# Softcap attention and spectral mix on one core: the second tanh behind the first transposes' rounding, and the last output block in halves

## The chip, the cores and the metric

The kernel runs on 1 core of one Trainium2 chip. The metric is device microseconds of one execution, as the median of several runs. The engines are named as the profile names them: PE is TensorE (its weight loads are PEld), DVE is VectorE, ACT is ScalarE, POOL is GpSimd, SP is SyncE, which here issues the DMA transfers.

## The reference

Attention with a soft cap, 8 batches of 12 heads, 448 positions, 64 per head, followed by a layer that mixes positions and channels (the names with `moe_` are this layer's):

```
scores = (q @ k.T) / sqrt(64)
scores = cap * tanh(scores / cap)                  # cap = 30
attn   = exp(scores - max); attn = attn / (sum(attn) + 1e-9)
x      = attn @ v                                  # to [8, 448, 768]
theta  = x @ w_theta
zr, zi = x * cos(theta), x * sin(theta)
u      = x + w_tok_r @ zr + w_tok_i @ zi           # over positions
out    = u + max(u @ w_ch, 0)
```

All inputs and outputs are float32, up to the products with `w_theta`, the tokens' weights and `w_ch`, which the kernel makes from high and low parts.

## The kernel before, in words

Everything is kept transposed, channels on partitions and positions along the row. The heads are taken in pairs: a pair k (48 in all, 6 per batch) fills one block of 128 channels, `X[b, j]`.

The outermost loop, in `pipeline`, runs over slots s. The first 8 slots (`FIRST`) hold attention alone. After them six slots make a batch b of the second layer; `part`, 0 to 5, is the slot's place among the six. In each slot s below 48 (`live`) the kernel also does the attention of pair s, so that both kinds of work are interleaved. The program is scheduled by hand: each engine executes its instructions in the order in which the Python code emits them, and waits on semaphores where a tile isn't ready. PE, DVE, ACT and the DMA issues on SP are thus four queues, each in order. What an instruction at the head of a queue waits for delays everything behind it in that queue.

A slot goes like this:

- `qk_half(s, 0)`: the score products of the first half of the keys (PE, line 217) into the tile `s`, which has one buffer of four PSUM banks, and then their tanh (ACT, line 219) into `p`.
- `av(s - 1)`: the product with v of the pair before (line 257, into a bank of the pool `psM`), copied by ACT (line 260).
- `sums`: the row sums `r` (line 273) of the two pairs before, in a bank of `psM`; `invert` takes their reciprocal (DVE, line 296), spreads it by four DMAs (line 300), and `norm` multiplies later (line 304).
- `qk_half(s, 1)`: the second half of the scores and their tanh. The scores' buffer is the one that the first half had.
- the script of the part, a list of steps. The letters A and B are the exponentials of the two halves (line 225), a and b the additions of their parts (lines 247, 250).

The script of the third part, `part == 2`, is the one that matters here:

```
[(transp, 1), (sincos, 1), (mix, 0), (rotate, 3), (transp, 2), "A", (mix, 1), "a", (rotate, 4), (transp, 3), "B",
 (mix, 2), "b", (rotate, 5)],
```

`transp(b, j)` transposes a rotated block in seven pieces (PE, line 355) into two banks `t`; ACT copies each to `zh`, rounded (line 356), and DVE forms the remainder `zl` (line 357), which frees the bank. `mix(b, j)` accumulates 21 products of `zh` and `zl` (lines 364 to 366) in a bank `mx`, and DVE adds the result to X (line 367). `sincos` is two ACT instructions (lines 341, 342) with a load of the activation table ahead of them, and `rotate(b, j)` a multiplication on DVE (line 346). The pool `psM` has four banks for all of these.

In the third part `invert(s - 1)` is emitted after the script's first step, `transp(b, 1)`, and so is `prep(s + 1)`, which rounds the next q and k on DVE (lines 193, 194) and issues the load of those after it (line 183). In the other parts both come ahead of the script. Third parts with `live` true are the seven slots s = 10, 16, 22, 28, 34, 40 and 46; in all seven s - 1 is odd, so that `invert` has work to do.

At the end of a batch, `chan(b, m)` makes the product with `w_ch` for one output block (lines 322 to 324), and one DVE instruction takes the maximum with zero and adds (line 375); SP stores the block (line 376). The last block of the last batch is the last work of the kernel.

Of the kernel before, what the change touches and what calls it, by code (L numbers as in the profile page):

```python
# [16 lines left out]
AF = mybir.ActivationFunctionType  # L17
ALU = mybir.AluOpType

P = 128  # L20
# [12 lines left out]
WHOLE = 14  # L33
# [3 lines left out]
def softcap_attn_then_spectral_mix(ctx, tc, qk2, v, cap, w_theta, w_tok, w_ch, ident, outT):  # L37
    nc = tc.nc
    B, NP, P, _, S = qk2.shape
    D = P // 2  # L40
    CP = v.shape[2]
    NCH = S // CP
    DM = NP * P
    NJ = DM // P
    NC2 = 2 * S // P
    NS = B * NP
# [14 lines left out]
    qscale = const.tile([P, 1], F32, name="qscale")  # L61
# [20 lines left out]
    def fill(n):  # L82

        t = psM.tile([P, 512], F32, tag="m", name=f"fill{len(fills)}")
        fills.append(t)
        for _ in range(n):
            nc.tensor.matmul(t[:32, :CP], ones_sb, ones_sb[:, :1].broadcast_to([CP, CP]), start=True, stop=True)
# [77 lines left out]
    def weights(s, pos):  # L165
        for word in WEIGHTS.get((s, pos), "").split():
            step = steps[word[-3:-1], int(word[-1])]
            {">": step.load, "*": step.scale, "#": step.vscale}.get(word[0], step.split)()
# [8 lines left out]
    def load_qk(k):  # L177

        if 0 < k < WHOLE:
            raw[k] = wk.tile([P, 2, S], F32, tag=("hi", "lo")[k % 2], name=f"qk{k}", bufs=1)  # L180
        else:
            raw[k] = qk_sb
        nc.sync.dma_start(raw[k], qk2[k // NP, k % NP])

    def load_v(k):
        vt[k] = wk.tile([CP, 2, NCH, D], F32, tag="v", name=f"v{k}", bufs=2)
        nc.sync.dma_start(vt[k], v[k // NP, k % NP])
# [10 lines left out]
    def apart(k):  # L198


        return k < NP and k % 2 == 0

    def qk_half(k, half):

        sp = psS.tile([P, 2, 2, 512], F32, tag="s", name=f"s{k}_{half}")
        if apart(k):
            pp = wk.tile([CP, 2, 2, S], F32, tag="xhl", name=f"p{k}_{half}", bufs=3)
        else:
            pp = wk.tile([CP, 2, 2, S], F32, tag="p", name=f"p{k}_{half}", bufs=3)
        pt[k, half] = pp  # L210
        for i in range(2):
            ks = slice((2 * half + i) * CP, (2 * half + i + 1) * CP)
            products = ((raw, raw),) if k < WHOLE else ((hi, hi), (lo, hi), (hi, lo))
            for n, (kk, qq) in enumerate(products):
                for hh in range(2):
                    rows = slice(hh * D, (hh + 1) * D)
                    nc.tensor.matmul(sp[:CP, i, hh, :S], kk[k][rows, 1, ks], qq[k][rows, 0, :],  # L217
                                     start=n == 0, stop=n == len(products) - 1)
        nc.scalar.activation(pp, sp[:CP, :, :, :S], AF.Tanh, scale=qscale[:CP])  # L219

    def exp_half(k, half):

# [29 lines left out]
    def av(k):  # L252
        va = vt.pop(k)
        acc = psM.tile([P, 512], F32, tag="m", name=f"a{k}")
        for c in range(NCH):
            for hh in range(2):
                nc.tensor.matmul(acc[hh * D : (hh + 1) * D, :S], va[:, hh, c, :], pt[k, c // 2][:, c % 2, hh, :],  # L257
                                 start=c == 0, stop=c == NCH - 1)
        x = wk.tile([P, S], F32, tag="x", name=f"x{k}", bufs=12)
        nc.scalar.copy(x, acc[:, :S])  # L260
        X[k // NP, k % NP] = x
# [24 lines left out]
    def invert(k):  # L286

        if k % 2 == 0:
            return
        r = state.pop("r")  # L290
        ri = wk.tile([P, S], F32, tag="ri", name=f"ri{k}", bufs=1)
        if state["general"]:
            nc.vector.tensor_scalar_add(ri, r[:, :S], 1e-9)
            nc.vector.reciprocal(ri, ri)
        else:
            nc.vector.reciprocal(ri, r[:, :S])  # L296
        for n in (k - 1, k):
            bc[n] = wk.tile([P, S], F32, tag="bc", name=f"bc{n}", bufs=2)
            for i in range(2):
                nc.sync.dma_start(bc[n][i::2, :], ri[D * (n % 2) : D * (n % 2) + D, :])  # L300

    def norm(k):
        x = X[k // NP, k % NP]
        nc.vector.tensor_tensor(x, bc.pop(k), x, op=ALU.mult)
# [4 lines left out]
    def split_x(b, j, name):  # L309
        if j % 2 == 0:  # L310
            state["xhl"] = wk.tile([P, 2, 2, S], F32R, tag="xhl", name=f"{name}{b}_{j}", bufs=3)
        t = state["xhl"][:, j % 2]
        nc.scalar.copy(t[:, 0, :], X[b, j])
        nc.vector.tensor_tensor(t[:, 1, :], X[b, j], t[:, 0, :].bitcast(F32), op=ALU.subtract)
        XHL[b, j] = t

    def proj(b, wh, wl, m, name):
        acc = psM.tile([P, 512], F32, tag="m", name=f"{name}{b}_{m}")
        ms = slice(m * P, (m + 1) * P)
        for j in range(NJ):  # L320
            t = XHL[b, j]
            nc.tensor.matmul(acc[:, :S], wh[:, j, ms], t[:, 0, :], start=j == 0, stop=False)  # L322
            nc.tensor.matmul(acc[:, :S], wh[:, j, ms], t[:, 1, :], start=False, stop=False)  # L323
            nc.tensor.matmul(acc[:, :S], wl[:, j, ms], t[:, 0, :], start=False, stop=j == NJ - 1)  # L324
        return acc
# [43 lines left out]
    def chan(b, m):  # L369
        acc = proj(b, wch_h, wch_l, m, "ch")  # L370
        if m == NJ - 1 and b + 1 < B:
            for j in range(NJ):
                split_x(b + 1, j, "xs")
        x = X.pop((b, m))
        nc.vector.scalar_tensor_tensor(x, acc[:, :S], 0.0, x, op0=ALU.max, op1=ALU.add)  # L375
        nc.sync.dma_start(outT[b, m * P : (m + 1) * P, :], x)

# [13 lines left out]
    def us(b, j):  # L393
        split_x(b, j, "us")

    def pipeline(general):
        state["general"] = general
        load_v(0)
        load_qk(1)
        for step in (("tk", 0), ("tk", 1)):  # L400
            steps[step].load()

        for s in range(FIRST + 6 * B):
            k = s - 1
            b, part = divmod(s - FIRST, 6)
            live = s < NS
            start = s < FIRST
            if s == 0:
                fill(FILL["first scores"])
            if live:  # L410
                qk_half(s, 0)
            if s == 0:
                fill(FILL["half"])
            if start:
                weights(s, "a")
                exp_half(s, 0)
            if 0 <= k < NS:
                av(k)
            if not start:
                weights(s, "a")  # L420
            if not start and part == 4:
                for j in range(NJ // 2, NJ):
                    us(b, j)
            if s + 1 < NS:
                load_v(s + 1)
            if 0 <= k < NS:
                sums(k, (0,) if start else (0, 1))
                if not start and part != 2:
                    invert(k)
            if live:  # L430
                qk_half(s, 1)
            if s == 0:
                fill(FILL["slot"])
            if 0 <= k and start:
                sums(k, (1,))
            if s + 2 <= WHOLE:
                load_qk(s + 2)
            if WHOLE <= s + 1 < NS and (start or part != 2):
                prep(s + 1)
            weights(s, "b")  # L440
            if 0 <= k and start:
                invert(k)
            script = ["B", "a", "b"] if start else part_scripts(b)[part]
            for i, e in enumerate(script):
                if not start and i == len(script) - 1:
                    weights(s, "c")
                    if s % 2 == 1 and s <= NS + 1:
                        norm(s - 3)
                        norm(s - 2)
                if isinstance(e, str):  # L450
                    if live:
                        if e in "AB":
                            exp_half(s, "AB".index(e))
                        else:
                            add_half(s, "ab".index(e))
                else:
                    e[0](b, e[1])
                if part == 2 and i == 0 and not start:
                    if 0 <= k < NS:
                        invert(k)  # L460
                    if WHOLE <= s + 1 < NS:
                        prep(s + 1)
            if start:
                weights(s, "c")
                for n in {4: (0, 1), 5: (2, 3), 7: (4, 5)}.get(s, ()):
                    norm(n)
                for j in {6: range(4), 7: range(4, NJ)}.get(s, ()):
                    split_x(0, j, "xs")
# [53 lines left out]
```

## Time and profile before

| | us |
|---|---|
| median of 3 runs | 964.53 (964.43 to 966.29) |
| profiled execution, its own time | 966.27 |
| its span, first to last instruction | 964.5 |
| PE busy | 945.6 |
| DVE busy | 640.8 |
| ACT busy | 590.5 |
| mean granted PE clock | 0.997 |

A profile page gives busy time per engine, the chain of work that ended last and groups of instructions by line. In a timeline a row has the start and the duration in us, the engine, the line of the kernel, the operation, what it writes and reads, its shape, how many instructions are merged in the row, and in brackets how long the engine had been idle before it and what ended that. Matmuls are pipelined and their ends are modelled, so that neighbouring ones overlap in the records.

### The profile page before, as it was taken

To read this page: it belongs to the slowest core of one execution; us is meant where nothing else is said; L and a number is where in the kernel's file an instruction comes from. 1 tells how busy PE (TensorE), PEld (TensorE's weight loads), DVE (VectorE), ACT (ScalarE), POOL (GpSimd) and SP (SyncE) were. 2 spreads that over 40 slices of the span, in tenths; PEclk is the share of its full clock that TensorE was granted. 3 is DMA by queue.
4 is the path that set the end of the run, shared out by engine and by line. 5 is a ranking of instruction groups with operands and counts; after the bars stand their busy time and mean duration, and the time that the engine had idled before them with its cause. 6 is when DMAs were issued, how large, how long until landed. Compare 5 with 4: busy or idle time off the path is not lost.

```text
span 964.5 us, 12776 instructions
## 1 busy us (share of the span) xinstructions
PE 945.6 (98%) x5224; PEld 697.3 (72%) x5224; DVE 640.8 (66%) x877; ACT 590.5 (61%) x609; POOL 0.4 (0%) x6
## 2 busy tenths in 40 slices
PE   8999999999999999999999999999999999999997
PEld 4234766677778777777787687767777877789897
DVE  5998787885855757756766559656585576664541
ACT  6888784667654687546963578456775558722520
POOL 0000000000000000000000000000000000000000
PEclk9999999999999999999999999999999999999999
DMA  7564122330113212132122221033011321001001
GB/s 252 193 194 138 34 82 94 112 103 30 49 39 105 67 39 63 32 98 67 32 66 68 77 67 48 29 87 94 31 49 39 105 68 39 20 15 62 0 1 61
DMA packets 30739, 68.68 MB, mean 71 GB/s; under 512 B 4304, under 2 KB 16720, under 8 KB 30672
## 3 DMA queue, kind: packets, MB, share of 16 engines
q1 hardware_dynamic: 30672, 67.78, 23.0%
q8 instruction: 43, 0.70, 0.3%
q14 instruction: 24, 0.20, 0.1%
HBM read 45.74 MB, written 11.01 MB: 59 GB/s over the span
## 4 chain that ended last, share of the span: by engine, by line
PE 88%; DVE 6%; ACT 4%; issue 1%; POOL 0%; POOLq 0%
PE a L257 15%; PE s L217 14%; PE mx L364 6%; PE mx L366 6%; PE mx L365 6%; PE th L322 6%; PE ch L322 6%; PE ch L324 6%; PE th L323 6%; PE ch L323 6%; PE th L324 6%; PE t L355 3%; PE r L273 3%; ACT p L219 2%; DVE ri L296 2%
## 5 line engine op out<-in xcount | busy, mean ns | idle before, releaser
L219 ACT ACTIVATE p<-s,qscale 112x1792 f32<-112x1792 f32 x96 | 168.7, 1757 | 168.7 <-PE s L217 168.7
L225 ACT ACTIVATE p<-p,cap_sb 112x1792 f32<-112x1792 f32 x96 | 170.6, 1790 | 0.6
L257 PE MATMUL a<-p,v 112*64 112x448 f32 x768 | 154.9, 545 | 0.0
L364 PE MATMUL mx<-wtk_h,zh 128*128 128x448 f32 x336 | 126.8, 377 | 5.4 <-DVE ri L296 3.6
L366 PE MATMUL mx<-wtk_h,zl 128*128 128x448 f32 x336 | 123.6, 368 | 0.0
L365 PE MATMUL mx<-wtk_l,zh 128*128 128x448 f32 x336 | 123.5, 367 | 0.0
L257 PEld LDWEIGHTS a<-p,v 112*64 112x64 f32 x768 | 50.9, 136 | 86.9 <-issue 77.1
L322 PE MATMUL th<-xs,wth_h 128*128 128x448 f32 x288 | 106.9, 371 | 0.0
L322 PE MATMUL ch<-us,wch_h 128*128 128x448 f32 x288 | 106.8, 371 | 0.0
L324 PE MATMUL ch<-us,wch_l 128*128 128x448 f32 x288 | 105.5, 366 | 0.0
L323 PE MATMUL th<-xs,wth_h 128*128 128x448 f32 x288 | 105.4, 366 | 0.0
L323 PE MATMUL ch<-us,wch_h 128*128 128x448 f32 x288 | 105.3, 366 | 0.0
L324 PE MATMUL th<-xs,wth_l 128*128 128x448 f32 x288 | 105.3, 366 | 0.0
L250 DVE TENSOR_TENSOR ps<-ps,p 112x896 f32<-112x896 f32 x80 | 87.0, 1087 | 1.4
L296 DVE RECIPROCAL ri<-r 128x448 f32<-128x448 f32 x24 | 70.8, 2952 | 12.0 <-PE r L273 11.9
L335 DVE SCALAR_TENSOR_TENSOR g_sb<-g_sb 128x448 f32<-128x448 f32 x48 | 29.9, 624 | 65.8 <-ACT g_sb L334 65.4
L364 PEld LDWEIGHTS mx<-wtk_h,zh 128*128 128x128 f32 x336 | 63.6, 189 | 11.9 <-issue 5.0
L357 DVE TENSOR_TENSOR zl<-t,zh 128x512 fp32r<-128x512 f32 x96 | 55.2, 616 | 24.5 <-ACT zh L356 24.5
L375 DVE SCALAR_TENSOR_TENSOR x<-ch,x 128x448 f32<-128x448 f32 x48 | 29.8, 620 | 59.0 <-PE ch L324 59.0
L366 PEld LDWEIGHTS mx<-wtk_h,zl 128*128 128x128 f32 x336 | 63.5, 189 | 5.4
L365 PEld LDWEIGHTS mx<-wtk_l,zh 128*128 128x128 f32 x336 | 63.7, 190 | 4.9
L322 PEld LDWEIGHTS ch<-us,wch_h 128*128 128x128 f32 x288 | 54.1, 188 | 9.6 <-issue 4.6
(75 smaller groups left out, 1377.8 us busy)
## 6 DMA issues: line engine op xcount, KB each, us to landing
qk_sb<-in_qk SPq DMA_DIRECT2D x35, 448.0 KB, 3.4
v<-in_v SPq DMA_DIRECT2D x48, 224.0 KB, 2.5
bc<-ri SPq DMA_DIRECT2D x96, 112.0 KB, 2.3
out_dram<-x SPq DMA_DIRECT2D x48, 224.0 KB, 1.9
qk<-in_qk SPq DMA_DIRECT2D x13, 448.0 KB, 3.4
g_sb<-in_wth SPq DMA_DIRECT2D x6, 768.0 KB, 5.4
g_sb<-in_wch SPq DMA_DIRECT2D x6, 768.0 KB, 4.7
swk_raw<-in_wtok SPq DMA_DIRECT2D x7, 448.0 KB, 4.1
```

What stands on the lines that cost most here:

```text
L217: nc.tensor.matmul(sp[:CP, i, hh, :S], kk[k][rows, 1, ks], qq[k][rows, 0, :], start=n == 0, stop=n == len(products) - 1)
L219: nc.scalar.activation(pp, sp[:CP, :, :, :S], AF.Tanh, scale=qscale[:CP])
L225: nc.scalar.activation(pp, pp, AF.Exp, scale=cap_sb[:CP])
L250: nc.vector.tensor_tensor(pst[k], pst[k], pt[k, 1][:, i], op=ALU.add)
L257: nc.tensor.matmul(acc[hh * D : (hh + 1) * D, :S], va[:, hh, c, :], pt[k, c // 2][:, c % 2, hh, :], start=c == 0, stop=c == NCH - 1)
L296: nc.vector.reciprocal(ri, r[:, :S])
L322: nc.tensor.matmul(acc[:, :S], wh[:, j, ms], t[:, 0, :], start=j == 0, stop=False)
L323: nc.tensor.matmul(acc[:, :S], wh[:, j, ms], t[:, 1, :], start=False, stop=False)
L324: nc.tensor.matmul(acc[:, :S], wl[:, j, ms], t[:, 0, :], start=False, stop=j == NJ - 1)
L364: nc.tensor.matmul(acc[:, :S], zh[:, c, :], wtk_h[:, c, :], start=c == 0, stop=False)
L365: nc.tensor.matmul(acc[:, :S], zh[:, c, :], wtk_l[:, c, :], start=False, stop=False)
L366: nc.tensor.matmul(acc[:, :S], zl[:, c, :], wtk_h[:, c, :], start=False, stop=c == NC2 - 1)
```

## The change

Two edits. First, `qk_half` no longer emits the tanh: it returns a function that does. The first half calls it at once, and so does the second half in most slots. In third parts (`late`) the tanh of the second half is emitted after the script's first step, so that in ACT's queue it stands behind the two copies of `transp(b, 1)`; `invert` and `prep` stay behind it in the emitted order. Second, the very last output block (b = 7, m = 5) is finished in two halves of 224 columns: DVE's instruction becomes two, the first half is stored by SP and the second by a DMA issued from ACT.

```
     def qk_half(k, half):
...
-        nc.scalar.activation(pp, sp[:CP, :, :, :S], AF.Tanh, scale=qscale[:CP])
+        return lambda: nc.scalar.activation(pp, sp[:CP, :, :, :S], AF.Tanh, scale=qscale[:CP])
...
     def chan(b, m):
...
-        nc.vector.scalar_tensor_tensor(x, acc[:, :S], 0.0, x, op0=ALU.max, op1=ALU.add)
-        nc.sync.dma_start(outT[b, m * P : (m + 1) * P, :], x)
+
+        parts = 2 if (b, m) == (B - 1, NJ - 1) else 1
+        for i in range(parts):
+            cs = slice(i * S // parts, (i + 1) * S // parts)
+            nc.vector.scalar_tensor_tensor(x[:, cs], acc[:, cs], 0.0, x[:, cs], op0=ALU.max, op1=ALU.add)
+            (nc.scalar if i else nc.sync).dma_start(outT[b, m * P : (m + 1) * P, cs], x[:, cs])
...
             if live:
-                qk_half(s, 0)
+                qk_half(s, 0)()
...
+            late = not start and part == 2
             if live:
-                qk_half(s, 1)
+                tanh = qk_half(s, 1)
+                if not late:
+                    tanh()
...
-            if WHOLE <= s + 1 < NS and (start or part != 2):
+            if WHOLE <= s + 1 < NS and (not late):
                 prep(s + 1)
...
-                if part == 2 and i == 0 and not start:
+                if late and i == 0:
+                    if live:
+                        tanh()
                     if 0 <= k < NS:
                         invert(k)
                     if WHOLE <= s + 1 < NS:
```

## The prediction

> **What bounds the kernel now.** I read the page first, for the engine that fills the span.
>
> ```profile
> span 964.5 us, 12776 instructions
> ...
> PE 945.6 (98%) x5224; PEld 697.3 (72%) x5224; DVE 640.8 (66%) x877; ACT 590.5 (61%) x609; POOL 0.4 (0%) x6
> ```
>
> TensorE (PE) is busy nearly throughout. A new order on ScalarE (ACT) can pay only where PE stands still, so I read next the list of waits.
>
> ```profile
> PE mx L364 <- DVE ri L296: 3.6, 7, 0.5
> ```
>
> Its columns are total us, times and longest: PE waits seven times, 0.51 us each, for the reciprocal of line 296. The change touches seven slots: s = 10, 16, ..., 46, the third parts that still have scores to compute. I then read the chain of waits in the slot s = 16 (start us, us, what).
>
> ```profile
> 245.17 0.94 ACT p L219
> 246.11 0.72 issue
> 246.83 0.58 ACT zh L356
> 247.41 0.02 issue
> 247.44 1.16 DVE zl L357 x2
> 248.59 2.87 DVE ri L296
> 251.46 0.14 issue
> 251.60 0.44 PE mx L364
> ```
>
> It goes from the tanh of the second scores (line 219) to the rounding of the transposes (356), their remainder on VectorE (DVE, 357), the reciprocal, and then PE's mix 1. By the order of releases mix 1 gets the PSUM bank that held the row sums, free only after the reciprocal has read it. The tanh heads this chain and has nothing to do with it: it is there because ACT works in order. The timeline of the same slot, engine by engine (ACT, DVE, PE), gives the slack.
>
> ```profile
> 245.17 1.76 ACT L219 ACTIVATE p<-s,qscale 112x1792 f32<-112x1792 f32 x1 [1.76 <-PE s L217]
> 246.83 0.95 ACT L356 CAST zh<-t 128x512 fp32r<-128x512 f32 x2
> 247.80 1.28 ACT L341 ACT_TABLE_LOAD   x1
> 249.09 1.42 ACT L341 ACTIVATE g_sb<-g_sb,quarter 128x1344 f32<-128x1344 f32 x1
> 250.42 1.31 ACT L342 ACTIVATE g_sb<-g_sb 128x1344 f32<-128x1344 f32 x1
> ...
> 256.59 0.97 ACT L356 CAST zh<-t 128x512 fp32r<-128x512 f32 x2 [0.91 <-PE t L355]
> ```
>
> ```profile
> 245.30 1.08 DVE L346 TENSOR_TENSOR g_sb<-g_sb,x 128x896 f32<-128x896 f32 x1
> 247.44 1.16 DVE L357 TENSOR_TENSOR zl<-t,zh 128x512 fp32r<-128x512 f32 x2 [1.05 <-ACT zh L356]
> 248.51 2.95 DVE L296 RECIPROCAL ri<-r 128x448 f32<-128x448 f32 x1
> ...
> 253.51 1.08 DVE L346 TENSOR_TENSOR g_sb<-g_sb,x 128x896 f32<-128x896 f32 x1
> 254.51 1.15 DVE L357 TENSOR_TENSOR zl<-t,zh 128x512 fp32r<-128x512 f32 x2
> ```
>
> ```profile
> 245.06 0.98 PE L355 MATMUL t<-ident_sb,g_sb 128*128 128x128 f32 x7
> ...
> 250.16 0.93 PE L355 MATMUL t<-ident_sb,g_sb 128*128 128x128 f32 x7
> ...
> 255.95 0.93 PE L355 MATMUL t<-ident_sb,g_sb 128*128 128x128 f32 x7
> 256.63 0.45 PE L364 MATMUL mx<-wtk_h,zh 128*128 128x448 f32 x1
> ```
>
> **What PE loses per slot.** Transposes followed by a mix without a wait: 256.63 - 255.95 = 0.68 us from start to start. With the wait: 251.60 - 250.16 = 1.44. The loss is 0.76, more than the 0.51 of shown idle, because modelled matmul ends cover part of it.
>
> **Part 1: tanh behind the rounding.** No instruction is added: the same tanh runs once per slot, after both zh copies instead of ahead of them.
>
> How early the copies can start: an unhindered copy follows its transposes by 256.59 - 255.95 = 0.64. The first transposes start at 245.06, so the copy comes at 245.70 instead of 246.83, 1.13 earlier. Its remainder could come 1.13 earlier too, but DVE is in the rotation of line 346 until 246.38; the row says DVE idled 1.05 for the copy, so it gains 1.05. The reciprocal follows directly and now ends at 251.46 - 1.05 = 250.41; with the 0.14 of issue mix 1 may go at 250.55. Unhindered it would go at 250.16 + 0.68 = 250.84. The wait is gone with 0.29 to spare: gain 0.76.
>
> In s = 10 DVE has more to do and less to win.
>
> ```profile
> 130.82 1.16 DVE L357 TENSOR_TENSOR zl<-t,zh 128x512 fp32r<-128x512 f32 x2 [0.48 <-ACT zh L356]
> ```
>
> Only 0.48 of idle lies ahead of the remainder there, so the reciprocal and mix 1 come 0.48 earlier. I take the other six as the slot s = 16. Sum: 6 x 0.76 + 0.48 = 5.04 us.
>
> What gets late is the tanh. It starts at 245.70 + 0.97 (pitch of the two copies, 247.80 - 246.83) = 246.67 instead of 245.17. Behind it on ACT stand the table load, cosine, sine, the copies of transposes 2 and the exponentials. With the pitches of the rows, 1.66 for the tanh (246.83 - 245.17), 1.29, 1.33 and 1.31 for the last, the sine ends at 252.26 instead of 251.73, 0.53 later. Its consumer, rotation 3 on DVE at 253.51, itself moves up 1.06 to 252.45: it still finds the sine done, by 0.2. PE has more slack: rotation 3 may start as late as 255.87 (new mix 2) - 0.14 - 1.15 (remainder) - 1.00 (rotation pitch, 254.51 - 253.51) = 253.58 before mix 2 waits for its remainder. The cover is 253.58 - 252.26 = 1.32 us; beyond it PE would wait at mix 2. The tanh's own readers are later still: it now ends near 248.4, while exponential B comes behind the copies of 256.59, and the score bank's next writer is the next slot. DVE's rounding of the next q and k behind the reciprocal, SP's stores of the reciprocal and the q-k load behind them are issued earlier by up to the 1.05; nothing in SP's queue is added or passed, and POOL has no part in it. The bank order is unchanged, since the tanh takes and frees no bank of that pool.
>
> **Part 2: the last block in halves.** VectorE's one operation becomes two of 224 columns; the first half is stored by SP, the second by ACT's queue. Every issue that the page lists is SP's, so a store from ACT is bounded by SP's. The rows are the timeline's end, the last store's time from issue to landing, the group of the same kind of operation at 768 columns, the page's row of a 112 KB transfer, and the shortest, median and longest landing of the last six stores.
>
> ```profile
> 959.41 0.62 DVE L375 SCALAR_TENSOR_TENSOR x<-ch,x 128x448 f32<-128x448 f32 x1 [3.04 <-PE ch L324]
> 960.07 0.33 SPq L376 DMA_DIRECT2D out_dram<-x  x1
> ```
>
> ```profile
> DMA to landing us min/median/max: 2.6/2.6/2.6
> ```
>
> ```profile
> L121 DVE SCALAR_TENSOR_TENSOR g_sb<-g_sb 128x768 int32<-128x768 int32 x12 | 11.5, 961 | 0.4
> ```
>
> ```profile
> bc<-ri SPq DMA_DIRECT2D x96, 112.0 KB, 2.3
> ```
>
> ```profile
> DMA to landing us min/median/max: 1.9/2.2/3.7
> ```
>
> From 0.62 us at 448 columns to 0.961 at 768: 1.07 ns a column, so 0.38 for 224. Two of them end at 959.41 + 0.76 = 960.17 instead of 960.03, 0.14 later. With the same 0.04 to the issue, the second half is issued at 960.21. With the 2.3 of the 112 KB row it lands at 962.51, against 960.07 + 2.6 = 962.67 now: gain 0.16. The ends: with 1.9 it lands at 962.11 (-0.6), with 3.7 at 963.91 (+1.2). I take 2.3 because the size is the same. The first half, issued 0.24 earlier, is hidden behind the second.
>
> The Trainium skill (DMA: Bandwidth & Descriptors, Rules for kernel authors) speaks against this part: two halves of a transfer share the same 16 DMA engines, and a second issuing engine saves only issue time, so "Don't bother". Its halves are halves of the partitions; here they are columns, but the engines are shared all the same. By that rule this part gives 0 and the whole change 5.0. No run here shows yet which.
>
> **The sum.** 5.04 + 0.16 = 5.2 us. The profiled execution took 966.27 for a span of 964.5 and becomes about 961.1 for a span of 959.3. The median of the runs is 964.53, 1.7 below the profiled execution's time (one of the three runs was 966.29), so the forecast of the median is 964.53 - 5.2 = 959.3. Should the median fall on an execution of the longer kind, it is 961.1.
>
> **Rivals.**
>
> Partial gain: only the shown idle comes back, 7 x 0.51 = 3.6, because the other 0.25 per slot is PE's own restart, or because the copies come later after their transposes than 0.64. With the tail as forecast this gives 960.8, with its worst end, +1.2, it is 962.1. For it: the 0.29 to spare at mix 1 is small. Against it: transposes and mix without a wait stand 0.68 apart, all restart included.
>
> No change: mix 1 waits for something else that comes at the same time, so that only the tail moves: 964.4. For it: a wait is put down to what came last, and another could stand just behind. Against: what else mix 1 reads, the remainder of the first transposes, is done 2.87 us before (it ends where the reciprocal starts), and the sine on ACT, at 251.73, ends after mix 1 has started.
>
> Slower: the tanh between the copies and the sine brings two additional table loads per slot on ACT.
>
> ```profile
> L341 ACT ACT_TABLE_LOAD x15 | 19.2, 1283 | 0.3
> L225 ACT ACT_TABLE_LOAD x14 | 18.0, 1283 | 0.3
> ```
>
> Two loads of 1.283 put the sine's end at 252.26 + 2.57 = 254.83, the remainder of transposes 2 at 255.83 to 256.98 and mix 2 at 257.12, 0.49 after its place now; in seven slots 3.4, so 964.53 + 3.4 - 0.16 = 967.8. It decides once ACT is late by more than 254.34 - 252.26 = 2.1 us in each slot (254.34 is the start of rotation 3 that lets mix 2 go at 256.63, as now). Against it: the sines and what follows them have 15 and 14 loads in the whole kernel, so tanh, copy and exponential need none between them, and the new order has copies and tanh together ahead of the sine's load.
>
> **How the numbers follow.** Forecast 0.80 (its own range, with the tail's ends, 958.9 to 960.7), partial gain 0.11, no change 0.04, slower 0.05. A difference under 0.2% (1.9 us) can't be told from none in this kernel. Forecast and partial gain are both faster by more than that: 0.91; same 0.04; slower 0.05. The range runs from 957.8, a little more gain than the 0.76 per slot, to 961.9: it takes in a median of the longer kind and most of the partial gain.
>
> **What would show it.** Right: no wait of mix 1 (364) on the reciprocal; the copy (356) of the first transposes 0.64 after their start, the tanh behind it; the remainder right behind rotation 2, and the reciprocal behind it; transposes 2 to mix 1 at 0.68; as many table loads as before; the two last issues about 0.37 apart and the span's end 4.2 us after the last VectorE operation, now 4.5 (964.5 - 960.03). Wrong would be: PE waiting on line 357 or 346 in these slots (ACT's cover gone), a copy that comes over 0.3 later after its transposes, or a last store that takes 3.7.

## The result and the profile after

The kernel after takes 959.57 us in the median of 4 runs (959.22 to 959.83), beside 965.41 for the kernel before on the same chip (4 runs, 964.43 to 966.36): ratio 0.9936, interval 0.9922 to 0.995. The prediction was 959.3. The profiled span went from 964.5 to 958.1 us, 6.4 us, where the sum had 5.2; the difference is a second matter, told below.

The list of waits of the kernel after has one row left for mix products on PE; the seven waits on the reciprocal (296) are gone.

```profile
PE mx L364 <- DVE zl L357: 1.8, 1, 1.8
```

The timeline of the slot s = 16, as ACT, DVE and PE lines, shows the new order.

```profile
245.56 0.97 ACT L356 CAST zh<-t 128x512 fp32r<-128x512 f32 x2 [2.35 <-PE t L355]
246.41 1.77 ACT L219 ACTIVATE p<-s,qscale 112x1792 f32<-112x1792 f32 x1
248.20 1.28 ACT L341 ACT_TABLE_LOAD   x1
249.49 1.42 ACT L341 ACTIVATE g_sb<-g_sb,quarter 128x1344 f32<-128x1344 f32 x1
250.82 1.31 ACT L342 ACTIVATE g_sb<-g_sb 128x1344 f32<-128x1344 f32 x1
```

```profile
245.10 1.08 DVE L346 TENSOR_TENSOR g_sb<-g_sb,x 128x896 f32<-128x896 f32 x1
246.18 1.16 DVE L357 TENSOR_TENSOR zl<-t,zh 128x512 fp32r<-128x512 f32 x2
...
247.25 2.95 DVE L296 RECIPROCAL ri<-r 128x448 f32<-128x448 f32 x1
...
252.26 1.08 DVE L346 TENSOR_TENSOR g_sb<-g_sb,x 128x896 f32<-128x896 f32 x1
```

```profile
244.87 0.98 PE L355 MATMUL t<-ident_sb,g_sb 128*128 128x128 f32 x7
...
249.96 0.93 PE L355 MATMUL t<-ident_sb,g_sb 128*128 128x128 f32 x7
250.65 0.45 PE L364 MATMUL mx<-wtk_h,zh 128*128 128x448 f32 x1
...
255.01 0.93 PE L355 MATMUL t<-ident_sb,g_sb 128*128 128x128 f32 x7
255.69 0.45 PE L364 MATMUL mx<-wtk_h,zh 128*128 128x448 f32 x1
```

The copies start 0.69 us after their transposes (245.56 - 244.87) and the tanh follows. The remainder (357) no longer has an idle time in brackets: it comes right behind rotation 2. The reciprocal ends at 250.20, and mix 1 follows transposes 2 by 0.69 (250.65 - 249.96) where it was 1.44: the gain is 0.75 in this slot. In s = 10 it is less:

```profile
133.94 0.93 PE L355 MATMUL t<-ident_sb,g_sb 128*128 128x128 f32 x7
134.82 0.45 PE L364 MATMUL mx<-wtk_h,zh 128*128 128x448 f32 x1
```

0.88 from start to start there, 0.57 less than the 1.45 before (133.54 to 134.99). The end of the kernel, as the timeline and the last stores' time to landing show it:

```profile
953.09 0.69 DVE L379 SCALAR_TENSOR_TENSOR x<-ch,x 128x224 f32<-128x224 f32 x2 [3.04 <-PE ch L324]
953.51 0.33 SPq L380 DMA_DIRECT2D out_dram<-x  x1
953.81 0.38 ACTq L380 DMA_DIRECT2D out_dram<-x  x1
```

```profile
DMA to landing us min/median/max: 2.7/2.7/2.7
```

From VectorE's last start to the span's end it takes 958.1 - 953.09 = 5.0 us, and took 964.5 - 959.41 = 5.1.

**Where 6.4 us went.** PE's place in the two traces, at points that can be compared (transposes of s = 10 in; third transposes of s = 46; third transposes of s = 52, in the last batch), before in the first fence and after in the second:

```profile
128.44 0.98 PE L355 MATMUL t<-ident_sb,g_sb 128*128 128x128 f32 x7
...
829.45 0.92 PE L355 MATMUL t<-ident_sb,g_sb 128*128 128x128 f32 x7
...
912.75 0.93 PE L355 MATMUL t<-ident_sb,g_sb 128*128 128x128 f32 x7
```

```profile
128.84 0.98 PE L355 MATMUL t<-ident_sb,g_sb 128*128 128x128 f32 x7
...
824.68 0.93 PE L355 MATMUL t<-ident_sb,g_sb 128*128 128x128 f32 x7
...
906.42 0.93 PE L355 MATMUL t<-ident_sb,g_sb 128*128 128x128 f32 x7
```

The kernel after comes into the first of the seven slots 0.40 late; its trace first records the full clock at 10.69 us, the one before at 9.87, and 0.82 us more at half clock would cost 0.41 (an estimate). At the end of the last slot it is 4.77 early: the slots gave 5.17 (predicted 5.04). Between the last two points it gains another 1.56, in a stretch that the change does not touch. The tail gives 0.1. The 1.56 is a stretch of half clock in the trace before. In the table of windows of the kernel before (us, then busy time of PE, PEld, DVE, ACT and POOL with their instructions, granted clock, DMA):

```profile
904.16:907.58 3.42, 1.59 (x12) 1.30 (x11) 2.82 (x6) 3.42 (x7) 0.00 (x0) 1.00 0.00 0
907.58:910.99 3.41, 3.41 (x11) 3.02 (x10) 1.72 (x3) 1.33 (x2) 0.00 (x0) 0.50 0.00 0
910.99:914.40 3.41, 3.41 (x22) 3.17 (x21) 1.45 (x2) 0.97 (x2) 0.00 (x0) 1.00 0.00 0
```

PE stands idle for 1.83 us in the first window, ahead of mix 0 of s = 52 (the row of the first fence, in both kernels). In the second the granted clock is 0.50, and half as many matmuls run (11 instead of 22). In the profile of the kernel after the same idle runs from 900.21 to 902.04, and the clock stays at 1.00:

```profile
898.15:901.56 3.41, 2.06 (x17) 1.74 (x15) 2.42 (x5) 2.81 (x7) 0.00 (x0) 1.00 0.00 0
901.56:904.97 3.41, 2.93 (x14) 2.72 (x15) 2.96 (x5) 2.57 (x3) 0.00 (x0) 1.00 0.00 0
```

The changes of clock in a trace lie on a grid of 3.41 us. In the kernel before the idle lay whole within one interval of it; here a boundary at 901.56 cuts it. So 1.56 of the 6.4 us are the luck of these two executions and not of the change. The two times of the kernel before, which the prediction had noticed (964.5 and 966.3) without a cause, lie about as far apart.

### The profile page after: what moved, and what is told of

Same layout as the page of the kernel before. It is cut to its first block, busy times and chain, and to the rows that moved or that the text cites. A ratio compares the mean times of both kernels' runs of the same rounds, so it can differ in the third digit from the quotient of the medians.

```text
span 958.1 us, 12772 instructions
## 1 busy us (share of the span) xinstructions
PE 942.8 (98%) x5224; PEld 696.7 (73%) x5224; DVE 641.7 (67%) x878; ACT 589.8 (62%) x609; POOL 0.4 (0%) x6
## 4 chain that ended last, share of the span: by engine, by line
PE 93%; ACT 3%; DVE 3%; issue 1%; POOL 0%; POOLq 0%
PE a L257 15%; PE s L217 14%; PE mx L364 7%; PE mx L366 7%; PE mx L365 7%; PE th L322 6%; PE ch L322 6%; PE ch L324 6%; PE th L324 6%; PE th L323 6%; PE ch L323 6%; PE t L355 4%; PE r L273 3%; ACT p L219 2%; PE fill L87 1%
## 5 line engine op out<-in xcount | busy, mean ns | idle before, releaser
L379 DVE SCALAR_TENSOR_TENSOR x<-ch,x 128x448 f32<-128x448 f32 (+1 forms) x49 | 29.8, 611 | 59.1 <-PE ch L324 59.1
L356 ACT CAST zh<-t 128x512 fp32r<-128x512 f32 x96 | 45.8, 532 | 31.1 <-PE t L355 31.1
```

## The experiments

**The tanh alone.** The kernel after with the last block stored whole:

```
-        parts = 2 if (b, m) == (B - 1, NJ - 1) else 1
+        parts = 1
```

> Only the tanh is moved; the last block is stored whole. My theory (the wait of mix 1 on the reciprocal cost 0.76 us in six slots and about 0.5 in one, and the halves are worth 0.1): 4.9 to 5.1 us under the kernel before where both run at full granted clock, so 959.4 to 959.7, no wait of line 364 on line 296, and the span's end 5.08 us after VectorE's last operation starts, as before. Rival, the halves bring the 1.2 us by which the profiled spans differ beyond my sum: 960.5 or more.

Measured 960.59 (5 runs, 959.33 to 961.27), ratio to the kernel before 0.9947 (0.9933 to 0.9961). Three runs with a mean granted clock of 0.997 took 960.59 to 961.27, and the profiled one of these has a half clock window in its trace. One, at 0.999, took 959.81, a tenth above the forecast; one, at 0.998, took 959.33 and can't be placed without its trace. So the median alone (960.59, just where the rival begins) decides little, and the trace decides: transposes of s = 10 start at 127.86 and the third ones of s = 46 at 823.76, 0.58 and 5.69 ahead of the kernel before. The seven slots gave 5.11 without the halves, and 5.17 with them. There is no wait of 364 on 296. The span ends 5.2 us after VectorE's last start (953.76, span 959.0).

**The halves alone.** The kernel before, with the changed end of `chan`.

> Only the last block is cut in halves; the tanh stays ahead of the copies. My theory: within 0.2 us of the kernel before (964.4 or so at full clock), VectorE's last start to the span's end 5.0 us instead of 5.08. Rival, the halves bring 1.2 us: 963.3.

Measured 966.16 (11 runs, 964.39 to 966.64), ratio 1.0006 (0.9997 to 1.0016), against a kernel before at 966.0 (23 runs, 962.95 to 966.65). The rival's 1.2 us is excluded; a gain of 0.16 is neither shown nor excluded, since the interval reaches from 0.3 us less to 1.5 us more, and ten of the eleven runs have the lower clock (0.997) beside thirteen of the 23. The span ends 5.2 us after VectorE's last start (957.50, span 962.7). In all ten profiles of this document that time is 5.08 to 5.20 with the store whole (three kernels, median 5.10) and 4.73 to 5.22 with it in halves (seven kernels, median 4.96): if the halves gain a tenth, it is smaller than the scatter.

**The tanh twice.** The kernel after, with the late tanh executed twice:

```
                     if live:
                         tanh()
+                        tanh()
```

> The kernel after, with the late tanh executed twice in the seven slots (the second writes the same values). ACT is 1.66 us later in each. My cover arithmetic on the trace after: rotation 3 may start up to 253.40 in the slot s = 16, the sine ends at 252.13, so the cover is 1.27; 1.66 exceeds it by 0.4, PE waits 0.4 us at mix 2 in six slots and 0.2 in s = 10: 2.6 us over the kernel after, about 962.1, with waits of line 364 on line 357. Rival, ACT has slack to spare in these slots (61% busy): no change, 959.5. Other rival, everything of ACT is on the path: 7 x 1.66 = 11.6, 971.

Measured 962.65 (7 runs, 962.31 to 963.51). That is 3.1 us over the kernel after's 959.57, where 2.6 was expected. The profiled execution took 962.31 with a span of 960.5, only 2.4 us over the kernel after's 958.1, both without a half clock window; but it comes into the slot s = 10 0.74 ahead of the kernel after (128.10 and 128.84) and leaves the third transposes of s = 46 2.15 behind it (826.83 and 824.68), so that the seven slots lost 2.9 us up to there, and with the last slot's wait at mix 2, which stands behind that point, 3.3. In the slot s = 16:

```profile
253.54 1.09 DVE L346 TENSOR_TENSOR g_sb<-g_sb,x 128x896 f32<-128x896 f32 x1 [1.61 <-ACT g_sb L342]
254.55 1.15 DVE L357 TENSOR_TENSOR zl<-t,zh 128x512 fp32r<-128x512 f32 x2
254.68 0.42 PEld L355 LDWEIGHTS t<-ident_sb,g_sb 128*128 128x128 f32 x4 [0.30 <-DVE g_sb L346]
254.69 1.15 PE L355 MATMUL t<-ident_sb,g_sb 128*128 128x128 f32 x7
...
255.75 0.19 PEld L364 LDWEIGHTS mx<-wtk_h,zh 128*128 128x128 f32 x1 [0.15 <-DVE zl L357]
255.75 0.47 PE L364 MATMUL mx<-wtk_h,zh 128*128 128x448 f32 x1
```

Rotation 3 now waits 1.61 us for the sine; PE waits a little for rotation 3 and then for the remainder (transposes 3 to mix 2: 255.75 - 254.69 = 1.06 instead of 0.68). That is the wait and the place that the cover arithmetic gave, and nearly the size: 0.38 at mix 2 and 0.1 at the transposes, where 0.4 was expected. The extra tanh delays ACT by 1.79 us (the load stands at 249.58 behind two tanhs that start at 246.00) and not by the 1.66 that I had taken, and 1.79 less the cover of 1.27 is 0.52. Neither rival (0 or 11.6 us) holds.

**The tanh and a half.** The same with `tanh(1)` behind `tanh()`, which repeats only the first of the two key blocks of the half.

> The kernel after with one and a half tanhs in the seven slots (the extra half writes the same values): ACT about 0.95 us later in each. The cover is 1.27, so nothing is lost: 959.5 at full clock. Rival, ACT's lateness costs in proportion (the doubled tanh cost 2.4 us of span): 960.8.

Measured 959.5 (4 runs, 957.54 to 959.91); the profiled span is 958.1, as without the extra half, and the seven slots cost PE the same to 0.1 us. In the slot s = 16 rotation 3 waits 0.86 us for the sine, but the transposes behind it still have their mix 0.68 later: the lateness reaches DVE and not PE. Within the cover, ACT time in these slots is free.

**The rounding of q and k first.** The kernel after, with two steps exchanged:

```
-                    if 0 <= k < NS:
-                        invert(k)
                     if WHOLE <= s + 1 < NS:
                         prep(s + 1)
+                    if 0 <= k < NS:
+                        invert(k)
```

> The kernel after with the next q and k rounded (lines 193, 194) ahead of the reciprocal in the third parts instead of behind it; the tanh stays late. My theory (mix 1 gets the bank that the reciprocal frees, so the reciprocal's end decides, not the tanh): in six slots the reciprocal ends 1.6 us later, 251.81 in the slot s = 16, and mix 1 goes at 251.95 instead of 250.65: 6 x 1.3 = 7.8 us, 967.3, with waits of line 364 on line 296. Rival, mix 1 waited for the remainder or the copies, which are as early as in the kernel after: 959.5.

Measured 969.1 (6 runs, 967.29 to 969.72), ratio 1.0034 (1.0019 to 1.0049). The one run at a mean clock of 0.999, 967.63, is 0.3 above the forecast; the others, at 0.997 and 0.998, took 967.29 to 969.72, and the profiled one of these, 969.41, has a half clock window in its trace. From the transposes of s = 10 (128.80) to the third ones of s = 46 (832.92) it loses 8.3 us against the kernel after, where 7.8 was expected. The wait is back, in the six slots that round q and k; its row in the list of waits, and DVE and PE in the slot s = 16:

```profile
PE mx L364 <- DVE ri L296: 6.7, 6, 1.1
```

```profile
248.88 2.95 DVE L296 RECIPROCAL ri<-r 128x448 f32<-128x448 f32 x1
...
251.98 0.45 PE L364 MATMUL mx<-wtk_h,zh 128*128 128x448 f32 x1 [1.11 <-DVE ri L296]
```

The copies and the remainder are as early here as in the kernel after, and the tanh as late. So mix 1 is held by the reciprocal's end; the moved tanh helped only because the reciprocal stood behind the remainder, and the remainder behind the tanh.

**The idle ahead of mix 0, filled.** The kernel before with small matmuls in the idle of s = 52, into the scores' bank:

```
+                if part == 2 and i == 0 and not live:
+                    t = psS.tile([P, 2, 2, 512], F32, tag="s", name="keep")
+                    for _ in range(12):
+                        nc.tensor.matmul(t[:32, 0, 0, :CP], ones_sb, ones_sb[:, :1].broadcast_to([CP, CP]), start=True, stop=True)
```

> The kernel before, with 12 small matmuls of constants into the idle scores' bank, in the one third part without scores after the last of the attention (s = 52), where PE stands idle for 1.83 us ahead of mix 0; their result is not used. Theory: the two times of the kernel before (964.4 and 966.3) differ by one 3.4 us window at half the granted clock that follows this idle when it falls whole into one window; 3.41 x 0.5 = 1.7 us. With the fill the idle is cut, the granted clock stays at 1.0 there, and all runs are at 964.4 to 964.9, none at 966.3, while the kernel before keeps showing both. Rival, the two times have another cause (transfers at the start, the store at the end): both still appear, in about half of the runs each.

Measured 965.03 (11 runs, 963.33 to 965.75), ratio 0.9992 (0.9983 to 1.0001). All eleven runs have a mean granted clock of 0.999. Of the 23 runs of the kernel before beside them, thirteen have 0.997; twelve took 966.0 to 966.65, ten 964.12 to 964.73 and one 962.95. With the idle filled no run has the lower clock, so the rival falls. (Two runs are shorter than the rest, 963.33 and 963.54; this is the last section's matter.) I had its time too low, 964.4 to 964.9: the fill is longer than the idle, and mix 0 starts 4.09 us after its transposes instead of 3.52.

```profile
903.14 1.69 PE L355 MATMUL t<-ident_sb,g_sb 128*128 128x128 f32 x14
904.76 2.53 PE L461 MATMUL keep<-ones_sb 112*32 112x112 f32 x24
907.23 0.47 PE L364 MATMUL mx<-wtk_h,zh 128*128 128x448 f32 x1
```

**The kernel after again.**

> The kernel after once more. Theory: it still has the 1.83 us idle of PE in the last batch's third part (s = 52), so it too has two times, 959.5 at full granted clock and about 961.2 where that idle falls whole into one 3.41 us window; by the windows' phase (1 - 1.83/3.41 = 0.46) in about half of the runs. Rival, the change has removed the slower of the two times: all runs at 959.2 to 959.9.

Measured 959.34 (5 runs): four from 958.98 to 959.47 and one, the profiled one, at 961.17 with a clock of 0.997. So the change has not removed the slower time, and the rival falls. That it came once in nine runs of this kernel, and in three of five with the tanh alone, is not the half that I expected; whether the change shifts how often the idle falls into one interval stays open.

The eight profiles that keep the idle can be set side by side. The interval is worked out from the changes of clock in each trace, in steps of 3.413 us:

| kernel | PE idle, us | interval in which it begins | half clock after it |
|---|---|---|---|
| before | 905.00 to 906.83 | 904.16 to 907.58 | yes |
| halves only | 903.05 to 904.88 | 902.06 to 905.47 | yes |
| tanh only | 899.30 to 901.12 | 898.95 to 902.36 | yes |
| after again | 899.67 to 901.50 | 899.30 to 902.72 | yes |
| q and k first | 908.45 to 910.28 | 908.28 to 911.69 | yes |
| after | 900.21 to 902.04 | 898.15 to 901.56 | no |
| tanh twice | 902.78 to 904.61 | 899.91 to 903.32 | no |
| tanh and a half | 900.06 to 901.89 | 897.71 to 901.13 | no |

In all five with a half clock window the idle lies whole within an interval; in all three without, a boundary cuts it.

For this idle the grid thus tells the two cases apart, but it does not make a rule for every idle. While there is attention alone, PE stands idle several times for 1.85 us ahead of score products. In each of the ten profiles at least one of these idle times lies whole within an interval of the same grid, with PE busy for 1.56 us of it, and the clock stays at full. In the kernel before it is the idle from 58.39 to 60.24:

```profile
57.66:61.07 3.41, 1.56 (x8) 0.45 (x6) 3.24 (x8) 2.87 (x3) 0.00 (x0) 1.00 0.85 238
61.07:64.48 3.41, 3.41 (x20) 1.24 (x18) 3.34 (x7) 3.40 (x3) 0.00 (x0) 1.00 0.56 182
```

That the idle of s = 52 brings on the half clock is shown by its filling; what sets it apart from the idle at 58.39, of the same length and as whole within its interval, stays open.

**The last theta's reduction behind the transposes.** The kernel after; in the last batch the reduction of the last theta is emitted behind the copies and remainders of the first transposes.

```
     def theta(b, j):
-        acc = proj(b, wth_h, wth_l, j, "th")
+        theta_acc[j] = proj(b, wth_h, wth_l, j, "th")
+        if (b, j) != (B - 1, NJ - 1):
+            reduce(b, j)
+
+    theta_acc = {}
+
+    def reduce(b, j):
+        acc = theta_acc.pop(j)
...
                     e[0](b, e[1])
+                    if e == (transp, 0) and b == B - 1:
+                        reduce(b, NJ - 1)
```

> The kernel after; in the last batch alone the last theta's reduction (lines 333 to 337) is emitted behind the first transposes' copies and remainders instead of ahead of them. Theory: mix 0 of s = 52 waits for the remainder, which waits behind that reduction; it comes 1.1 us earlier, PE's idle there falls from 1.83 to about 0.75, and the half clock window that follows it goes: 1.1 us under the kernel after's faster time, 958.4, in all runs. Rival, the later sine of the last batch is waited for instead: no gain, 959.5.

Measured 958.41 (5 runs, 958.25 to 958.51), ratio to the kernel before 0.9931 (0.9917 to 0.9945), the lowest median of all; beside it the kernel after had 959.34. The mean granted clock of the profiled execution is 1.000, and the five runs lie within 0.26 us. The gain over the kernel after's usual time is 0.9 where I expected 1.1; between the third transposes of s = 46 and those of s = 52 the two traces show 1.12 (80.62 us instead of 81.74). That no run has the lower clock says little by itself, as the kernel after had it in one of nine only. PE's wait there is now one of 0.74, for the copy that empties theta's bank for the second part of the next transposes:

```profile
900.46 0.55 PE L362 MATMUL t<-ident_sb,g_sb 128*128 128x128 f32 x3 [0.74 <-ACT g_sb L340]
900.76 0.45 PE L371 MATMUL mx<-wtk_h,zh 128*128 128x448 f32 x1
```

## Why the prediction was right, point by point

- The chain from the tanh over copy, remainder and reciprocal to mix 1: right. With the tanh moved the wait is gone, with or without the halves; with the reciprocal put 1.6 us later and the tanh left where it is, the wait is back.
- The price of a wait, taken from the start-to-start time and not from the shown idle: right. 0.75 was measured in s = 16, 0.76 predicted, and 0.51 is what the list of waits shows. The seven slots gave 5.17 in the profiles, 5.04 predicted; s = 10 gave 0.57 where its 0.48 of DVE idle was taken as the bound. The partial gain rival falls.
- The spare time at mix 1: predicted 0.29, measured 250.65 - 0.14 - 250.20 = 0.31.
- ACT's lateness: the sine ends at 252.13 (252.26 predicted on the time before), and rotation 3 finds it done by 0.13. The cover of 1.3 us is shown from both sides: an extra half tanh costs nothing, an extra whole one (1.79 us) costs 0.4 to 0.5 per slot. The term taken too small is the tanh's pitch ahead of the load, 1.66 predicted and 1.79 measured (246.41 to 248.20); it costs little here, since the tanh starts 1.54 us behind its transposes where 1.61 was forecast: from the transposes to the sine's end it is 7.26 us, 7.20 predicted. No table load was added, so the slower rival did not occur.
- The tail: 0.16 predicted; 0.1 in the profiles of before and after, and none to be seen in the pair with the halves alone. That the 0.1 is near the forecast is luck. The step mis-sized is the landing: the halves of the kernel after take 2.7 us each, not the 2.3 of the 112 KB rows, so that the smaller size bought no time (in all profiles the second half takes 2.4 to 2.9, a whole store 2.3 to 2.6). The last landing comes 0.2 later after VectorE's start than before; what made the tail shorter is the time between that landing and the end of the span, 1.6 instead of 1.8 us, which the prediction had left as it was and whose cause is not known. The rule of the Trainium skill (DMA: Bandwidth & Descriptors, Rules for kernel authors), that two halves of a transfer share the engines and aren't worth it, agrees with these runs, in which halves by columns gain nothing that can be told from nothing.
- What the prediction lacked: the cause of the two times of the kernel before. It took the shorter as its base, as the median of three stood there, and named 961.1 as the other possibility. That all four runs of the kernel after were of the shorter kind, and so the median within 0.3 of the forecast, is luck: later one run of this kernel took 961.17, and with the tanh alone three of five were of the longer kind. The median before in the comparison, 965.41, lies between the two times, so the measured difference of 5.8 us holds part of the half clock window. From the shorter time (964.43 and 964.53) to 959.57 it is 4.9, beside 5.2 predicted.

## What to carry to other kernels

On an engine that works in order, look at what heads the chain into a wait: an instruction that nobody needs soon can sit ahead of one that the bound engine is waiting for, and exchanging the two costs nothing as long as the lateness stays within the cover behind it (here 1.3 us, worked out beforehand and tested by executing the instruction once and a half and twice). Price a wait on PE by the start-to-start time against the same pair without a wait. When the runs of a kernel fall into groups, look for a dip of the granted clock and for the idle in front of it before comparing medians. For what a change is worth, compare the same two places in both traces: two spans can differ by what happened ahead of the change and behind it (here by 0.40 and 1.56 us).

## What the runs showed of the hardware

An idle time of PE of 1.83 us, ahead of mix 0 of s = 52, was followed by a window of 3.41 us at half clock in the five profiles in which it fell whole into one interval of a 3.41 us grid (PE was busy for 1.59 of 3.42 us in the kernel before), and in none of the three in which a boundary cut it (2.06 busy of 3.41 in the kernel after). Filling it kept the clock at full in eleven of eleven runs. It is no rule for every idle: in each of the ten profiles at least one idle of 1.85 us in the stage of attention alone lay whole within an interval, with 1.56 busy of 3.41, and the clock stayed at full. The grid's place against the kernel's start differs from run to run (in two profiles of the kernel after, an interval begins at 898.15 and at 899.30), which makes two times of one program, 1.7 us apart. The Trainium skill (TensorE: Matmul & The Clock Gate, What's actually happening) gives a free-running window of 3413 ns and the two clocks, and the traces agree; but it speaks of an idle window and (HAM oscillation) of idle gaps above about 3.4 us, and here a gap of half that length was enough in five profiles.

A few runs of several kernels are shorter still by 1.4 us or so (962.95 and 963.13 of the kernel before, 957.54 of the tanh and a half). No profile was taken of these, but the profile of the halves alone shows what can do it. Its run took 964.50 although it has the half clock window; it enters s = 10 1.90 us ahead of the kernel before (126.54 and 128.44). Its clock is first recorded at full at 4.35 us, those of the other nine profiles at 8.07 to 10.69, and its first score products on PE take half the time that they take in the kernel before. The row of the halves alone, and the one of the kernel before:

```profile
5.34 1.76 PE L217 MATMUL s<-qk_sb 64*112 64x448 f32 x8 [0.28 <-DMA qk_sb<-in_qk]
```

```profile
5.36 3.33 PE L217 MATMUL s<-qk_sb 64*112 64x448 f32 x8
```

So a time near 964.4 can also be a run with the half clock window and an early clock, and the mean clock has to be read beside the time.
